# One transfer of 14 rows per partition for W_down in a decode block of attention and a gated feed-forward

## The chip, the cores and the metric

The kernel runs on one core of a Trainium2 chip. A core has a matrix engine (PE, whose weight loads the profile lists apart as PEld), a vector engine (DVE), a scalar engine (ACT), GpSimd (POOL), and a sync engine (SP) that here only starts transfers. Sixteen DMA engines move data between the device memory and the core's on-chip memory, which has 128 partitions. The metric is the device time of one execution in microseconds (us); lower is better. Before the change it is 198.91 us, the median of three runs (198.54 to 199.20).

## The reference

The block adds three things: the input, an attention over a window of a cache, and a gated feed-forward. For four batch rows and one query position each:

```
xn  = layernorm(x)                                  # x: 4 x 512
q   = (xn @ wq) as 32 heads of 128
k,v = the last W = 4096 positions of the caches     # 8 KV heads, 4 query heads each
o   = softmax(q k^T / sqrt(128)) v                  # per batch row and head
A   = o (4 x 4096) @ wo                             # wo: 4096 x 512
B   = (silu(xn @ w_gate) * (xn @ w_up)) @ w_down    # w_gate, w_up: 512 x 1792, w_down: 1792 x 512
out = x + A + B
```

All inputs and the output are bf16. The windows of the two caches are 8 x 4 MB each (4 batch rows, 4096 positions, 128 values), the weights wq and wo 4 MB each, and the three feed-forward matrices 1.75 MB each.

## The kernel before

**The order of the transfers.** SP starts all the large loads on one queue, which the 16 DMA engines work through in order. First come wq, w_gate and w_up, then the keys and values of eight passes, one KV head each for all four batch rows (K0, K1, V0, K2, V1, ... K7, V6, V7), and last w_down and wo. Keys and values have two buffers each: K(r) is started when the transposes of pass r-2 are done (the wait of L232, seen at the start on L233), V(r) when the product with the values of pass r-1 is done (L237, seen on L238). w_down has no wait of its own. It goes into the memory of w_gate and w_up, which were used up at the start. wo goes into the first key buffer in five pieces (`ROWS`: rows 0-15, 16-21, 22-28, 29-30 and 31 of the 32 rows per partition), and its first piece waits until the last keys of that buffer are transposed (L257).

**The start.** While these loads run, DVE and ACT normalize x. PE multiplies by wq (L469), then by w_gate and w_up (L485). PE's result for the feed-forward is laid out in four strips of 32 output partitions, `k` = 0 to 3. Each strip holds up to four tiles of the 1792 hidden values, and the columns of a tile are taken with a stride from the weight's row, because the tile's position on 128 partitions must fit the rows of w_down later. ACT and DVE form silu(gate) * up (L270, L323 to L330), PE transposes the four tiles at once (L490), and DVE copies them into `guT` (L334, L335), which waits in memory for the rest of the kernel. PE goes on to the first pass after `guT` is done (L493).

**A pass.** PE transposes 128 key tiles (L417), DVE and ACT copy them out of PE's result memory (L342, L274), PE forms scores (L426), DVE their maximum (L346), ACT the exponential (L277), PE the sums (L519) and the product with the values (L435).

**The end.** After the last pass PE transposes and regroups the attention's result (L560, L564). Then it adds three products in one result buffer `part_ps`, again in four strips: x, w_down (L574), and the first 22 of 32 row groups of wo (L581). ACT and DVE copy the buffer out (L280, L392), PE folds the four strips into one result (L586) and adds the last ten row groups of wo to it (L593), DVE converts (L394), and SP stores (L260).

**w_down's two parts.** The matrix has 1792 rows = 14 x 128. The kernel before takes the first 1536 rows as 12 rows on each of 128 partitions (`WDA`, one transfer, 12 KB per partition), and the other 256 rows as four rows on each of 64 partitions (`WDB`, two transfers of 32 partitions, 4 KB per partition). So the last strip of the gate and up products has tiles of 64 columns, and the last four products of L574 add over 64 partitions only.

Of the kernel before, what the change touches and what calls it, by code (L numbers as in the profile page):

```python
# [3 lines left out]
BF16 = mybir.dt.bfloat16  # L4
# [6 lines left out]
def bass_parallel_sum__sliding_block_cached__swiglu_ffn__decode_kernel(  # L11
# [12 lines left out]
    B, _, D = A_x.shape  # L24
    _, HKV, Sk, Dh = A_k_cache.shape
    HQ = A_wq.shape[1] // Dh
    F = B_w_gate.shape[1]
# [8 lines left out]
    NC = D // 128  # L36
    NF = F // 128
    REP = HQ // HKV
    CQ = B * REP
    LAST = HKV  # L40

    TA, TB2, PB = 12, 4, 64
    assert 128 * TA + PB * TB2 == F
    SCALE = float(Dh) ** -0.5
    EPS = 1e-5
    BIG = 1.0e30
# [3 lines left out]
    sb = nc.alloc_sbuf_tensor  # L50
# [2 lines left out]
    VB = [sb("vbuf%d" % s, [128, NT, Dh], BF16) for s in range(2)]  # L53
    WG = sb("wg_sb", [128, NC, F], BF16)
    WU = sb("wu_sb", [128, NC, F], BF16)
    WDA = WG[:].rearrange("p c n -> p (c n)")[:, 0:TA * D].rearrange("p (t n) -> p t n", n=D)
    WDB = WU[:].rearrange("p c n -> p (c n)")[:, 0:TB2 * D].rearrange("p (t n) -> p t n", n=D)
    WO = KB[0][:].rearrange("p t d -> p (t d)").rearrange("p (j n) -> p j n", n=D)
    WQ = VB[1][:].rearrange("p t d -> p (t d)").rearrange("p (c n) -> p c n", c=NC)

# [6 lines left out]
    XnT = sb("xnT", [128, NC, 32], BF16)  # L67
# [17 lines left out]
    OT = sb("oT", [128, HKV + 1, CQ], BF16)  # L85
    Rn = sb("rn", [128, 128], BF16)
    OP = sb("oP", [128, 32, 32], BF16)
    guT = sb("guT", [128, TA + TB2, 32], BF16)
    part = sb("part", [128, D], FP32)
    y = sb("y_sb", [128, 128], BF16)  # L90

# [21 lines left out]
    gate_ps = ps_S[2]  # L113
    up_ps = ps_S[3]
    qT_ps = kt_ps[1]
    gT_ps = kt_ps[0][:, 0:4, :]
    part_ps = ps_S[0]
# [4 lines left out]
    def sem(name):  # L122
        return nc.alloc_semaphore(name=name)
# [3 lines left out]
    d_v = [sem("d_v%d" % g) for g in range(2)]  # L127
    d_wg = sem("d_wg")
    d_wu = sem("d_wu")
    d_wda = sem("d_wda")  # L130
    d_wdb = sem("d_wdb")
    d_wo = [sem("d_wo%d" % q) for q in range(len(ROWS))]
    d_out = sem("d_out")
    s_const = sem("s_const")
# [42 lines left out]
    wq_ap = A_wq.rearrange("(p c) n -> p c n", c=NC)  # L177
    wg_ap = B_w_gate.rearrange("(p c) n -> p c n", c=NC)
    wu_ap = B_w_up.rearrange("(p c) n -> p c n", c=NC)
    wda_ap = B_w_down[0:128 * TA, :].rearrange("(p t) n -> p t n", t=TA)  # L180
    wdb_ap = B_w_down[128 * TA:, :].rearrange("(p t) n -> p t n", t=TB2)
    wo_ap = A_wo.rearrange("(p j) n -> p j n", j=32)

    BY_ACT = (4, 7, 8, 11, 12, 14)
# [44 lines left out]
    def run_sync(eng):  # L229
        def load_k(r):  # L230
            if r >= 2:
                eng.wait_ge(s_tr[NCH - 1], r - 1)  # L232
            eng.dma_start(KB[r % 2][:].rearrange("p t d -> p (t d)"), kv_ap(A_k_cache, r)).then_inc(d_k[r % 2], 16)  # L233

        def load_v(r):
            if r:
                eng.wait_ge(s_pv, r)  # L237
            eng.dma_start(VB[r % 2][:].rearrange("p t d -> p (t d)"), kv_ap(A_v_cache, r)).then_inc(d_v[r % 2], 16)  # L238

        eng.dma_start(WQ[:], wq_ap).then_inc(d_v[1], 16)  # L240
        eng.dma_start(WG[:], wg_ap).then_inc(d_wg, 16)
        eng.dma_start(WU[:], wu_ap).then_inc(d_wu, 16)
        load_k(0)
        load_k(1)
        load_v(0)
        for r in range(2, HKV):
            load_k(r)
            load_v(r - 1)
        load_v(HKV - 1)
        eng.dma_start(WDA, wda_ap).then_inc(d_wda, 16)  # L250

        for u in range(0, PB, 32):
            eng.dma_start(WDB[u:u + 32].rearrange("p t n -> p (t n)"),  # L253
                          wdb_ap[u:u + 32].rearrange("(e p) t n -> e p (t n)", p=4)).then_inc(d_wdb, 16)
        for q, (a, b) in enumerate(ROWS):
            if q == 0:
                eng.wait_ge(s_tr[NCH - 1], HKV - 1)  # L257
            eng.dma_start(WO[:, a:b, :], wo_ap[:, a:b, :]).then_inc(d_wo[q], 16)
        eng.wait_ge(s_y, 1)
        eng.dma_start(out_ap, y_ap).then_inc(d_out, 16)  # L260
        eng.wait_ge(d_out, 16)
# [20 lines left out]
    def run_vector(eng):  # L282
# [2 lines left out]
        nc.regs_mov(nx, 0)  # L285
        loc = eng.mark_branch_hint_location()
        eng.memset(XnT[:], 0.0)
        for t in (gate_ps, up_ps):
            eng.memset(t[96:128, :].rearrange("p (t m) -> p t m", m=128)[:, :, PB:], 0.0)
        eng.wait_ge(d_x, 16)  # L290
        eng.tensor_reduce(st_sum[:], X[:], AX.X, ALU.add)
        eng.drain()
# [38 lines left out]
        eng.wait_ge(s_gt, 1)  # L331
        eng.wait_ge(s_fill, 1)
        gT = gT_ps.rearrange("p t (k e) -> p k t e", e=32)
        eng.tensor_copy(guT[:, 0:TA, :].rearrange("p (k t) e -> p k t e", t=4), gT[:, 0:3])  # L334
        eng.tensor_copy(guT[0:PB, TA:, :], gT[0:PB, 3, 0:TB2, :])  # L335
        eng.drain().then_inc(s_guT, 1)
        for t in s_xp + [s_nm]:
            eng.sem_inc(t, 1)
# [57 lines left out]
    def run_tensor(eng):  # L396
        mm = eng.matmul
# [54 lines left out]
        with nc.body("t_head", valid_engines=me):  # L452
            loc = eng.mark_branch_hint_location()
            for t, v in ((nx, 1), (odd, 0), (nk[0], 16), (nk[1], 16)):
                nc.regs_mov(t, v)
            eng.wait_ge(s_c2, 1)
            eng.wait_ge(s_xn, 1)
            for c in range(NC):
                last = eng.transpose(xT_ps[:, c * B:(c + 1) * B],  # L459
                                     xn[:].rearrange("b (p c) -> b c p", c=NC)[:, c, :], ident[0:B, 0:B])  # L460
            last.then_inc(s_xT, 1)
            eng.wait_ge(s_const, 1)
            mm(mask_ps, Lsel[:], Dsh[:])
            eng.wait_ge(s_xnT, 1)
            eng.wait_ge(d_v[1], 16)
            for c in range(NC):
                for j in range(2):
                    for k in range(4):
                        last = mm(ps_S[j][32 * k:32 * k + 32, :], XnT[:, c, :],  # L469
                                  WQ[:, c, 512 * (4 * j + k):512 * (4 * j + k) + 512],  # L470
                                  start=(c == 0), stop=(c == NC - 1), skip_group_check=True)
            last.then_inc(s_q, 1)
            eng.wait_ge(s_qs, 2)
            for j in range(2):
                for h in range(4):
                    last = eng.transpose(qT_ps[:, 4 * j + h, :], qs[:, j, 128 * h:128 * h + 128], ident[:])
            last.then_inc(s_qt, 1)
            for w, d, o, s_w in ((WG, d_wg, gate_ps, s_g), (WU, d_wu, up_ps, s_u)):
                wa = w[:, :, 0:128 * TA].rearrange("p c (m t) -> p c t m", t=TA)
                wb = w[:, :, 128 * TA:].rearrange("p c (m t) -> p c t m", t=TB2)  # L480
                eng.wait_ge(d, 16)
                for c in range(NC):
                    for k in range(4):
                        v = wb[:, c] if k == 3 else wa[:, c, 4 * k:4 * k + 4, :]
                        last = mm(o[32 * k:32 * k + 32, :].rearrange("p (t m) -> p t m", m=128)[:, 0:v.shape[1], 0:v.shape[2]],  # L485
                                  XnT[:, c, :], v, start=(c == 0), stop=(c == NC - 1), skip_group_check=True)
                last.then_inc(s_w, 1)
            eng.wait_ge(s_gu, 1)
            for t in range(4):
                last = eng.transpose(gT_ps[:, t, :], gu[:, 128 * t:128 * t + 128], ident[:])  # L490
            last.then_inc(s_gt, 1)
            eng.wait_ge(s_qc, 1)
            eng.wait_ge(s_guT, 1)  # L493
            nc.br("t_pass", engines=me)
# [20 lines left out]
        with nc.body("t_values", valid_engines=me):  # L515
            j = now(nx)
            for q in range(NB):
                eng.wait_ge(s_xp[q], j)
                last = mm(dn_ps[:], ones[:], P[:, q * TB:(q + 1) * TB, :].rearrange("p t c -> p (t c)"),  # L519
                          start=(q == 0), stop=(q == NB - 1))  # L520
# [11 lines left out]
        with nc.body("t_p_end", valid_engines=me):  # L532
            j = now(nx)
            eng.wait_ge(s_dd, j)
            for q in range(NB):
                mm(S_ps[q], Lsel[:], bc(Dsh[:], TB), start=False, stop=True,  # L536
                   skip_group_check=True).then_inc(s_sh[q], 1)
            eng.wait_ge(s_oc, j)
            for e in range(2):
                last = mm(ot_ps, o4[:, 128 * e:128 * e + 128], fold[:, 16 * e:16 * e + 16],  # L540
                          start=(e == 0), stop=(e == 1), skip_group_check=True)
# [16 lines left out]
        with nc.body("t_tail", valid_engines=me):  # L558
# [3 lines left out]
            for b in range(B):  # L562
                for q in range(4):
                    m = mm(op_ps[:, b, :], sel2[:, b, q, :], Rn[:, 32 * q:32 * q + 32],  # L564
                           start=(b == 0 and q == 0), stop=(q == 3), skip_group_check=True)
            m.then_inc(s_op, 1)
            eng.wait_ge(s_guT, 1)
            eng.wait_ge(d_wda, 16)
            for t in range(TA + TB2):
                k = (t + 1) % 4  # L570
                if t == TA:
                    eng.wait_ge(d_wdb, 16 * (PB // 32))
                a, w = (guT[:, t, :], WDA[:, t, :]) if t < TA else (guT[0:PB, t, :], WDB[0:PB, t - TA, :])
                mm(part_ps[32 * k:32 * k + 32, :], a, w, start=(t < 3), stop=False, skip_group_check=True)  # L574
            eng.wait_ge(s_opc, 1)
            for j in range(EARLY):
                for q, (a, b) in enumerate(ROWS):
                    if a == j:
                        eng.wait_ge(d_wo[q], 16)
                k = (j + 3) % 4  # L580
                m = mm(part_ps[32 * k:32 * k + 32, :], OP[:, j, :], WO[:, j, :], start=False,  # L581
                       stop=(j >= EARLY - 4), skip_group_check=True)
            m.then_inc(s_pt, 1)
            eng.wait_ge(s_ptc, 2)
            for n in range(NC):
                mm(acc_ps[32 * n:32 * n + 32, 0:128], fold[:], part[:, 128 * n:128 * n + 128],  # L586
                   start=True, stop=False, skip_group_check=True)
            for j in range(EARLY, 32):
# [3 lines left out]
                for n in range(NC):  # L592
                    m = mm(acc_ps[32 * n:32 * n + 32, 0:128], OP[:, j, :], WO[:, j, 128 * n:128 * n + 128],  # L593
                           start=False, stop=(j == 31), skip_group_check=True)
# [6 lines left out]
    run_sync(nc.sync)  # L601
    run_scalar(nc.scalar)
    run_vector(nc.vector)
    run_tensor(nc.tensor)


# [26 lines left out]
```

## Time and profile before

| What | Value |
|---|---|
| Median of three runs | 198.91 us (198.54 to 199.20) |
| The profiled execution's own time | 198.22 us |
| Its span (first to last instruction) | 197.0 us |
| Mean granted PE clock | 0.948 of full speed |
| PE busy | 155.0 us (79%) |
| PE weight loads busy | 121.2 us (62%) |
| DVE busy | 114.6 us (58%) |
| ACT busy | 68.8 us (35%) |
| POOL busy | 10.8 us (5%) |
| The SP queue's packets, share of 16 engines' span | 97.0%, 81.01 MB |
| Mean rate of all transfers | 412 GB/s |

The profile is one execution, so stretches of it are compared with its own span; the time of the execution is 1.22 us longer than the span. Line numbers (L574) are those of the kernel before. "Idle" in a row is the time an engine stood still just before, and behind the arrow stands what released it. A busy PE is not PE at its peak, because matmuls are pipelined. In rows of stretches the columns are the length, the busy time and instruction count of each engine, the granted PE clock, the mean busy share of the 16 DMA engines, and the rate that they moved. A packet's busy time runs from its start to its end, so that the share can exceed 1 where packets of one engine overlap.

### The profile page before, as it was taken

What the parts mean: (1) busy time and instruction counts of PE and PEld (TensorE: products, weight loads), DVE (VectorE), ACT (ScalarE), POOL (GpSimd) and SP (SyncE); (2) the same over time, 40 slices, a digit from 0 to 9 for tenths busy, and PEclk for the clock granted to TensorE, in tenths of its full rate; (3) what the DMA queues carried; (4) which work ended last, traced back from release to release, by engine and by line L of the source; (5) the groups of instructions that cost most, each with busy time, mean ns of one, the idle gap of its engine ahead of it and who ended that gap; (6) DMA issues with size and microseconds to landing.
All of it is one profiled execution on the core that took longest, in us unless ns stands there. A gap on an engine that the chain in (4) does not pass through costs nothing.

```text
span 197.0 us, 6539 instructions
## 1 busy us (share of the span) xinstructions
PE 155.0 (79%) x2926; PEld 121.2 (62%) x2926; DVE 114.6 (58%) x218; ACT 68.8 (35%) x86; POOL 10.8 (5%) x27
## 2 busy tenths in 40 slices
PE   0038936998998999899899985998599879988444
PEld 0012106986786888689688954885598568755112
DVE  5472373667667586776768664765376756752201
ACT  2003100470563456057246512652156046430001
POOL 8750000000000000000000000000000000000000
PEclk9999975699999999999999999999799999999957
DMA  6999999999999999999999999999999999999991
GB/s 214 439 427 425 472 453 433 416 433 429 423 423 426 426 426 433 426 426 426 426 439 439 433 439 446 439 426 439 426 433 426 426 426 426 433 411 349 370 400 46
DMA packets 3729, 81.09 MB, mean 412 GB/s; under 512 B 456, under 2 KB 588, under 8 KB 1036
## 3 DMA queue, kind: packets, MB, share of 16 engines
q1 hardware_dynamic: 3716, 81.01, 97.0%
q8 instruction: 5, 0.08, 0.2%
q10 hardware_dynamic: 8, 0.00, 0.0%
HBM read 81.01 MB, written 0.00 MB: 411 GB/s over the span
## 4 chain that ended last, share of the span: by engine, by line
DMA 45%; PE 41%; ACT 7%; DVE 3%; SPq 2%; issue 1%; DVEq 0%
DMA kbuf<-in_A_k_cache_dram 29%; PE ps_kt L417 21%; DMA kbuf<-in_A_wo_dram 15%; PE ps_s L426 9%; ACT kT L274 7%; PE ps_o L435 5%; PE ps_s L536 2%; DVE mxb L346 2%; PE ps_s L581 1%; PE ps_kt L523 1%; PE ps_o L540 1%; DVE mx L369 1%; PE ps_s L593 1%; DVE mxd L371 0%; SPq L253 0%
## 5 line engine op out<-in xcount | busy, mean ns | idle before, releaser
L417 PE MATMUL ps_kt<-ident,kbuf 128*128 128x128 bf16 x1024 | 72.3, 227 | 12.0 <-DMA kbuf<-in_A_k_cache_dram 8.5
L417 PEld LDWEIGHTS ps_kt<-ident,kbuf 128*128 128x128 bf16 x1024 | 61.9, 102 | 19.4 <-DMA kbuf<-in_A_k_cache_dram 9.0
L342 DVE COPY kT<-ps_kt 128x1024 bf16<-128x1024 bf16 x80 | 52.2, 687 | 22.8 <-PE ps_kt L417 21.9
L274 ACT COPY kT<-ps_kt 128x1024 bf16<-128x1024 bf16 x48 | 47.8, 1013 | 47.1 <-PE ps_kt L417 47.1
L277 ACT ACTIVATE p<-ps_s 128x512 bf16<-128x512 f32 x32 | 16.5, 603 | 43.5 <-PE ps_s L536 43.5
L346 DVE TENSOR_REDUCE mxb<-ps_s 128x16 f32<-128x512 f32 x32 | 22.1, 692 | 13.2 <-PE ps_s L426 11.6
L426 PE MATMUL ps_s<-qT,kT 128*128 x1024 | 29.4, 169 | 0.0
L426 PEld LDWEIGHTS ps_s<-qT,kT 128*128 128x128 bf16 x1024 | 27.8, 96 | 0.2
L435 PE MATMUL ps_o<-vbuf,p 128*32 128x256 bf16 x576 | 17.4, 273 | 1.3 <-DMA vbuf<-in_A_v_cache_dram 0.7
L435 PEld LDWEIGHTS ps_o<-vbuf,p 128*32 128x32 bf16 x576 | 15.1, 96 | 2.8 <-issue 2.4
L519 PE MATMUL ps_kt<-p,ones 128*128 128x512 bf16 x36 | 9.7, 378 | 0.2
L536 PE MATMUL ps_s<-dsh,lsel 128*128 128x512 bf16 x36 | 9.4, 382 | 0.0
L350 DVE TENSOR_REDUCE dsum<-ps_kt 128x16 f32<-128x512 f32 x9 | 6.2, 692 | 1.5 <-PE ps_kt L519 1.3
L356 DVE TENSOR_TENSOR oT<-ps_o,rden 128x16 f32 (+1 forms) x9 | 1.6, 175 | 8.9 <-PE ps_o L540 8.9
L469 PE MATMUL ps_s<-vbuf,xnT 128*32 128x512 bf16 x32 | 3.6, 629 | 3.6 <-DMA vbuf<-in_A_wq_dram 3.6
L523 PEld LDWEIGHTS ps_kt<-identf,mxd 128*128 128x128 f32 x9 | 1.2, 138 | 8.2 <-DVEq L372 8.2
L581 PE MATMUL ps_s<-kbuf,oP 128*32 128x512 bf16 x22 | 2.8, 623 | 4.4 <-DMA kbuf<-in_A_wo_dram 4.4
L523 PE MATMUL ps_kt<-identf,mxd 128*128 128x128 f32 x9 | 2.9, 322 | 4.3 <-DVEq L372 4.3
L540 PEld LDWEIGHTS ps_o<-fold,o 128*128 128x128 f32 x36 | 5.4, 190 | 1.3
L280 ACT COPY part<-ps_s 64x512 f32<-64x512 f32 x1 | 0.6, 580 | 14.8 <-PE ps_s L581 14.8
L459 PE MATMUL ps_s<-ident,xn 4*128 4x4 bf16 x4 | 0.3, 166 | 6.9 <-DVE xn L305 6.9
L392 DVE COPY part<-ps_s 64x512 f32<-64x512 f32 x1 | 0.7, 683 | 8.1 <-PE ps_s L581 8.1
(92 smaller groups left out, 77.9 us busy)
## 6 DMA issues: line engine op xcount, KB each, us to landing
kbuf<-in_A_k_cache_dram SPq DMA_DIRECT2D x8, 4096.0 KB, 26.9
vbuf<-in_A_v_cache_dram SPq DMA_DIRECT2D x8, 4096.0 KB, 28.8
vbuf<-in_A_wq_dram SPq DMA_DIRECT2D x1, 4096.0 KB, 12.3
kbuf<-in_A_wo_dram SPq DMA_DIRECT2D x1, 2048.0 KB, 30.4
wg_sb<-in_B_w_gate_dram SPq DMA_DIRECT2D x1, 1792.0 KB, 16.2
wu_sb<-in_B_w_up_dram SPq DMA_DIRECT2D x1, 1792.0 KB, 20.0
wg_sb<-in_B_w_down_dram SPq DMA_DIRECT2D x1, 1536.0 KB, 26.1
kbuf<-in_A_wo_dram SPq DMA_DIRECT2D x1, 896.0 KB, 33.5
```

The costliest lines, as they stand in the source:

```text
L274: eng.copy(KT[n % 8][:], kt_ps[n % 3]).then_inc(s_ev[n], 1)
L277: eng.activation(P[:, q * TB:(q + 1) * TB, :], S_ps[q], ACT.Exp, scale=SCALE).then_inc(s_xp[q], 1)
L342: eng.tensor_copy(KT[n % 8][:], kt_ps[n % 3]).then_inc(s_ev[n], 1)
L346: eng.tensor_reduce(mxb[:, q, :], S_ps[q].rearrange("p t c -> p c t"), AX.X, ALU.max)
L350: eng.tensor_reduce(dsum[:], dn_ps[:].rearrange("p (t c) -> p c t", c=CQ), AX.X, ALU.add)
L417: last = eng.transpose(kt_ps[n % 3][:, k, :], KB[g][:, 8 * n + k, :], ident[:])
L426: last = mm(S_ps[q][:, 8 * (n % 4) + k, :], KT[n % 8][:, k, :], QT[:, bass.ds(j, 1), :, :].rearrange("p o b h -> p (o b h)"), start=(n % 4 ...
L435: last = mm(o4_ps[32 * k:32 * k + 32, :], P[:, 2 * u:2 * u + 2, :].rearrange("p t c -> p (t c)"), VB[e][:, 2 * u:2 * u + 2, :].rearrange(" ...
L519: last = mm(dn_ps[:], ones[:], P[:, q * TB:(q + 1) * TB, :].rearrange("p t c -> p (t c)"), start=(q == 0), stop=(q == NB - 1))
L523: eng.transpose(mx_ps, mxd[:], identf[:]).then_inc(s_mt, 1)
L536: mm(S_ps[q], Lsel[:], bc(Dsh[:], TB), start=False, stop=True, skip_group_check=True).then_inc(s_sh[q], 1)
L540: last = mm(ot_ps, o4[:, 128 * e:128 * e + 128], fold[:, 16 * e:16 * e + 16], start=(e == 0), stop=(e == 1), skip_group_check=True)
```

## The change

w_down becomes one transfer: partition p takes the rows 14p to 14p+13, 14 KB in one piece, into the memory of w_gate alone. The two transfers onto 64 partitions and their semaphore are gone, and the 16 matmuls of L574 (12 over 128 partitions and 4 over 64) become 14 over 128.

The columns of the gate and up products follow: a tile is now every 14th column. The four strips take tiles 0-3, 4-7, 8-11 and 10-13, so that the last strip has 512 columns in place of 256 and computes tiles 10 and 11 a second time. DVE's two clears of the unused part of that strip (L289) are gone, and the second copy into `guT` takes the strip's last two tiles on 128 partitions in place of four tiles on 64.

```diff
-    TA, TB2, PB = 12, 4, 64
+    NF = F // 128
+    T0 = (0, 4, 8, NF - 4)
-    WDA = WG[:].rearrange("p c n -> p (c n)")[:, 0:TA * D].rearrange("p (t n) -> p t n", n=D)
-    WDB = WU[:].rearrange("p c n -> p (c n)")[:, 0:TB2 * D].rearrange("p (t n) -> p t n", n=D)
+    WD = WG[:].rearrange("p c n -> p (c n)").rearrange("p (t n) -> p t n", n=D)
-    wda_ap = B_w_down[0:128 * TA, :].rearrange("(p t) n -> p t n", t=TA)
-    wdb_ap = B_w_down[128 * TA:, :].rearrange("(p t) n -> p t n", t=TB2)
+    wd_ap = B_w_down.rearrange("(p t) n -> p t n", t=NF)
...
-        eng.dma_start(WDA, wda_ap).then_inc(d_wda, 16)
-        for u in range(0, PB, 32):
-            eng.dma_start(WDB[u:u + 32].rearrange("p t n -> p (t n)"),
-                          wdb_ap[u:u + 32].rearrange("(e p) t n -> e p (t n)", p=4)).then_inc(d_wdb, 16)
+        eng.dma_start(WD, wd_ap).then_inc(d_wd, 16)
...
-        for t in (gate_ps, up_ps):
-            eng.memset(t[96:128, :].rearrange("p (t m) -> p t m", m=128)[:, :, PB:], 0.0)
...
-        eng.tensor_copy(guT[:, 0:TA, :].rearrange("p (k t) e -> p k t e", t=4), gT[:, 0:3])
-        eng.tensor_copy(guT[0:PB, TA:, :], gT[0:PB, 3, 0:TB2, :])
+        eng.tensor_copy(guT[:, 0:12, :].rearrange("p (k t) e -> p k t e", t=4), gT[:, 0:3])
+        eng.tensor_copy(guT[:, 12:NF, :], gT[:, 3, 16 - NF:, :])
...
-                wa = w[:, :, 0:128 * TA].rearrange("p c (m t) -> p c t m", t=TA)
-                wb = w[:, :, 128 * TA:].rearrange("p c (m t) -> p c t m", t=TB2)
+                wt = w[:].rearrange("p c (m t) -> p c t m", t=NF)
...
-                        v = wb[:, c] if k == 3 else wa[:, c, 4 * k:4 * k + 4, :]
-                        last = mm(o[32 * k:32 * k + 32, :].rearrange("p (t m) -> p t m", m=128)[:, 0:v.shape[1], 0:v.shape[2]],
-                                  XnT[:, c, :], v, start=(c == 0), stop=(c == NC - 1), skip_group_check=True)
+                        last = mm(o[32 * k:32 * k + 32, :].rearrange("p (t m) -> p t m", m=128), XnT[:, c, :],
+                                  wt[:, c, T0[k]:T0[k] + 4, :], start=(c == 0), stop=(c == NC - 1), skip_group_check=True)
...
-            eng.wait_ge(d_wda, 16)
-            for t in range(TA + TB2):
+            eng.wait_ge(d_wd, 16)
+            for t in range(NF):
                 k = (t + 1) % 4
-                if t == TA:
-                    eng.wait_ge(d_wdb, 16 * (PB // 32))
-                a, w = (guT[:, t, :], WDA[:, t, :]) if t < TA else (guT[0:PB, t, :], WDB[0:PB, t - TA, :])
-                mm(part_ps[32 * k:32 * k + 32, :], a, w, start=(t < 3), stop=False, skip_group_check=True)
+                mm(part_ps[32 * k:32 * k + 32, :], guT[:, t, :], WD[:, t, :], start=(t < 3), stop=False,
+                   skip_group_check=True)
```

The order of SP's starts at the end of the kernel before, from V6 and V7 (L238) to the pieces of wo (L258); `wg_sb` and `wu_sb` are the memories of w_gate and w_up, and the shape behind a row is partitions x values:

```order
L238 DMA vbuf<-in_A_v_cache_dram 128x1x16384 x2
L250 DMA wg_sb<-in_B_w_down_dram 128x6144
L253 DMA wu_sb<-in_B_w_down_dram 32x2048 x2
L258 DMA kbuf<-in_A_wo_dram 128x8192
L258 DMA kbuf<-in_A_wo_dram 128x3072
L258 DMA kbuf<-in_A_wo_dram 128x3584
```

The same place after the change:

```order
L234 DMA vbuf<-in_A_v_cache_dram 128x1x16384 x2
L246 DMA wg_sb<-in_B_w_down_dram 128x7168
L250 DMA kbuf<-in_A_wo_dram 128x8192
L250 DMA kbuf<-in_A_wo_dram 128x3072
L250 DMA kbuf<-in_A_wo_dram 128x3584
```

Between the last values and the first piece of wo there is one start in place of three; the bytes are the same.

PE's matmuls at the end of the kernel before, from the transpose of the attention's result (L560) to the last rows of wo (L593):

```order
L560 MATMUL ps_kt<-ident,oT 128x128
L564 MATMUL ps_s<-rn,sel 128x32 x16
L574 MATMUL ps_s<-wg_sb,guT 32x512 x12
L574 MATMUL ps_s<-wu_sb,guT 32x512 x4
L581 MATMUL ps_s<-kbuf,oP 32x512 x22
L586 MATMUL ps_s<-part,fold 32x128 x4
L593 MATMUL ps_s<-kbuf,oP 32x128 x40
```

The same place after the change:

```order
L548 MATMUL ps_kt<-ident,oT 128x128
L552 MATMUL ps_s<-rn,sel 128x32 x16
L559 MATMUL ps_s<-wg_sb,guT 32x512 x14
L567 MATMUL ps_s<-kbuf,oP 32x512 x22
L572 MATMUL ps_s<-part,fold 32x128 x4
L579 MATMUL ps_s<-kbuf,oP 32x128 x40
```

The product with w_down is two matmuls shorter and reads one memory, behind one wait instead of two; nothing else has moved on PE.

More of the change, by code (lines that the diff above doesn't have):

```diff
@@ L40, in bass_parallel_sum__sliding_block_cached__swiglu_ffn__decode_kernel @@
     LAST = HKV
-    TA, TB2, PB = 12, 4, 64
-    assert 128 * TA + PB * TB2 == F
+    NF = F // 128
+    T0 = (0, 4, 8, NF - 4)
     SCALE = float(Dh) ** -0.5
@@ L87, in bass_parallel_sum__sliding_block_cached__swiglu_ffn__decode_kernel @@
     OP = sb("oP", [128, 32, 32], BF16)
-    guT = sb("guT", [128, TA + TB2, 32], BF16)
+    guT = sb("guT", [128, NF, 32], BF16)
     part = sb("part", [128, D], FP32)
@@ L129, in bass_parallel_sum__sliding_block_cached__swiglu_ffn__decode_kernel @@
     d_wu = sem("d_wu")
-    d_wda = sem("d_wda")
-    d_wdb = sem("d_wdb")
+    d_wd = sem("d_wd")
     d_wo = [sem("d_wo%d" % q) for q in range(len(ROWS))]
```

## The prediction

> **What bounds the kernel now.** I read the page first (the 40 slices and the chain), then the stretches of the end, then the transfers of single stretches. The slices say that the 16 DMA engines hardly rest:
>
> ```profile
> DMA  6999999999999999999999999999999999999991
> GB/s 214 439 427 425 472 453 433 416 433 429 423 423 426 426 426 433 426 426 426 426 439 439 433 439 446 439 426 439 426 433 426 426 426 426 433 411 349 370 400 46
> DMA 45%; PE 41%; ACT 7%; DVE 3%; SPq 2%; issue 1%; DVEq 0%
> ```
>
> A slice is 4.9 us. The rate stands near 426 GB/s for most of the kernel and falls in the last ones, to 349 and 370, although the engines stay 90% busy. The chain (third row) gives PE 41%, but it follows one path through a pipeline in which a pass of PE hides behind the transfers of the next; what all passes share is one queue that is never empty. So a byte saved or a stall removed on that queue should show, if the end of the kernel waits for it. Whether it does stands in the order of time:
>
> ```profile
> 178.95 1.93 PE L435 MATMUL ps_o<-vbuf,p 128*32 128x256 bf16 x64 [0.73 <-DMA vbuf<-in_A_v_cache_dram]
> 183.03 0.56 PE L564 MATMUL ps_s<-rn,sel 128*128 128x32 bf16 x16 [0.32 <-DVE rn L388]
> 183.77 0.83 PE L574 MATMUL ps_s<-wg_sb,guT 128*32 128x512 bf16 x12 [0.17 <-DMA wg_sb<-in_B_w_down_dram]
> 184.76 0.40 PE L574 MATMUL ps_s<-wu_sb,guT 64*32 64x512 bf16 x4 [0.17 <-DMA wu_sb<-in_B_w_down_dram]
> 189.59 2.82 PE L581 MATMUL ps_s<-kbuf,oP 128*32 128x512 bf16 x22 [4.42 <-DMA kbuf<-in_A_wo_dram]
> 191.37 0.13 PEld L581 LDWEIGHTS ps_s<-kbuf,oP 128*32 128x32 bf16 x6 [0.79 <-DMA kbuf<-in_A_wo_dram]
> 193.55 1.12 PEld L593 LDWEIGHTS ps_s<-kbuf,oP 128*32 128x32 bf16 x40 [0.17 <-DMA kbuf<-in_A_wo_dram]
> ```
>
> PE waits for the last values, then for w_down (by 0.17 us), and then 4.42 us for the first piece of wo, 0.79 us for the second and 0.17 us for the third. From 185.16 to the end the pace is that of wo's landing. w_down lies ahead of wo in the same queue, so what w_down costs the queue is passed on whole.
>
> **What w_down costs the queue.** Four stretches: the steady part, the arrival of w_down's first part, the five microseconds behind it, and one of wo alone.
>
> ```profile
> 160.00:176.00 16.00, 14.91 (x322) 12.45 (x320) 11.77 (x22) 6.38 (x7) 0.00 (x0) 1.00 0.99 428
> 176.00:180.00 4.00, 3.06 (x50) 1.88 (x53) 1.12 (x3) 1.66 (x4) 0.00 (x0) 1.00 0.92 387
> 180.00:185.00 5.00, 4.34 (x77) 2.53 (x66) 1.56 (x4) 0.00 (x0) 0.00 (x0) 1.00 1.04 316
> 185.00:189.00 4.00, 0.16 (x4) 0.00 (x0) 0.00 (x0) 0.00 (x0) 0.00 (x0) 0.84 0.96 403
> ```
>
> The last two numbers are DMA share and rate. From 180 to 185 us the engines are fully occupied (1.04) and move 316 GB/s, where they move 428 with as much occupation before. They don't lack work; each packet takes longer. The packets of three pieces of this stretch, 180 to 182, 182 to 185 and 185 to 186.8:
>
> ```profile
> DMA packets 106, 0.54 MB, mean 272 GB/s; under 512 B 35, under 2 KB 35, under 8 KB 82
> DMA packets 88, 1.04 MB, mean 345 GB/s; under 512 B 12, under 2 KB 12, under 8 KB 28
> DMA packets 47, 0.77 MB, mean 428 GB/s; under 512 B 0, under 2 KB 0, under 8 KB 0
> ```
>
> Between 2 and 8 KB lie 82-35 = 47 packets in the first and 28-12 = 16 in the second: 63 of the 64 packets of 4 KB that two transfers onto 32 partitions make. Where there are most, the rate is lowest (272); where there are some, 345; where there are none and the engines read wo alone, it is back at 428. So the slow stretch belongs to the 4 KB packets onto the 64 partitions, not to wo.
>
> **The change part by part.** (1) The queue. The same 1792 KB go out, in packets of 14 KB on all partitions; those of 4 KB vanish. The price of the slow stretch, first way: (428-316)/428 x 5 us = 1.31 us. Second way, by landings:
>
> ```profile
> 159.06 30.39 DMA kbuf<-in_A_wo_dram
> kbuf<-in_A_wo_dram SPq DMA_DIRECT2D x1, 2048.0 KB, 30.4
> wg_sb<-in_B_w_down_dram SPq DMA_DIRECT2D x1, 1536.0 KB, 26.1
> wu_sb<-in_B_w_down_dram SPq DMA_DIRECT2D x2, 128.0 KB, 25.0
> ```
>
> wo's first piece lands at 159.06+30.39 = 189.45, the last values at about 178.9 (PE's wait above ends there). Between the two go 1536+2x128+2048 = 3840 KB, 3.93 MB, in 10.55 us. At 428 GB/s they need 9.19, so 1.36 us are lost on the way to the landing that PE waits for. Both ways agree. The bounds: if 428 is too much for packets this small and 403 (the row of 185 to 189) is right, 3.93 MB need 9.76 us and 0.8 us are lost. Upward: from 176 to 180 the rate is 387, and with (428-387)/428 x 4 = 0.38 us added to 1.31 it is 1.7. The new packets have their like in this trace: w_gate and w_up are 14 KB on each of 128 partitions too, and the stretch in which they land shows no slow place:
>
> ```profile
> 13.00:21.00 8.00, 6.85 (x54) 2.29 (x56) 1.49 (x6) 1.87 (x2) 0.00 (x0) 1.00 1.07 457
> ```
>
> I take 1.3 us saved, bounds 0.7 to 1.7; the 0.7 is the first rival's.
>
> [...]
>
> (2) SP. Two starts fall away:
>
> ```profile
> 158.12 0.89 SPq L253 DMA_DIRECT2D wu_sb<-in_B_w_down_dram  x2
> 159.06 2.32 SPq L258 DMA_DIRECT2D kbuf<-in_A_wo_dram  x5
> ```
>
> wo's starts move up by 0.94 us, worth nothing: they land 30 us later, so they wait behind the queue. Without that cover (an empty queue) they would be worth the 0.94 us.
>
> (3) PE at the end. 14 matmuls at 0.83/12 = 0.069 us take 0.97 us, from 183.77 to 184.74. All of them now wait for the whole of w_down. Its 1792 KB need 4.29 us from 178.9, so it lands near 183.2, ahead of L564's end at 183.59. Behind this wait stands L581, which needs wo at about 189.45-1.3 = 188.15; so there are 3.4 us of cover, and the 0.4 us that PE ends earlier are worth nothing either.
>
> (4) After that, everything moves with wo. The second piece (L581's last six), the two copies, the fold and L593 keep their lengths, and each of the landings that start them comes 1.3 us earlier. L593 depends on wo's third piece and its last rows, all behind the same place in the queue. Half clock in the tail stays in the forecast (below).
>
> (5) The start. The last strip reads 512 columns in place of 256, in gate and up:
>
> ```profile
> L485 PE MATMUL ps_s<-wg_sb,xnT 128*32 128x512 bf16 x12 | 3.8, 1076 | 0.0
> L485 PE MATMUL ps_s<-wg_sb,xnT 128*32 128x256 bf16 x4 | 1.1, 414 | 0.0
> 29.14 0.21 DVE L335 COPY guT<-ps_kt 64x128 bf16<-64x128 bf16 x1
> 31.49 4.77 PE L417 MATMUL ps_kt<-ident,kbuf 128*128 128x128 bf16 x43 [2.67 <-DMA kbuf<-in_A_k_cache_dram]
> kbuf<-in_A_k_cache_dram SPq DMA_DIRECT2D x1, 4096.0 KB, 18.1
> 1.22 0.55 DVE L289 MEMSET ps_s<- 32x256 f32 x2
> ```
>
> Below: nothing, where the four strips run beside each other (12 of 1.08 us fit in 3.8). Above: 4 x (1076-414) = 2.65 us for each of the two. By columns it is 3.8 x (2048-1792)/1792 = 0.54 us each, and I take that. `guT` is ready at 29.35, the keys come at 31.49; so 2.1 us are covered. If the upper end came true for both (5.3 us), the first pass would start 3.2 us late at most, and the cover behind that is the queue: the keys started between 44 and 46 us (fifth row) land 18.1 us later though their 4.19 MB need 9.8, so they have 8.3 us of other bytes ahead. The longer stride (14 in place of 12 values) lies in the same bounds. The two clears on DVE (0.55 us, last row) lie ahead of its wait for x, and the copies keep their size. All of this: 0.
>
> Sum: -1.3 us. The profiled execution's span of 197.0 becomes 195.7, its own time of 198.22 becomes 196.9. The median of the runs is 0.69 us above that execution, so for the median I forecast 198.91-1.3 = **197.6 us**.
>
> **The rivals.** *Half of it.* Only the 4 KB packets themselves are slow, and the rest of the slow stretch is the switch from one kind of packet to the next, which stays. Then the gain is what the two microseconds with most of them lose, (428-272)/428 x 2 = 0.7 us: 198.2. For it speaks that the stretch from 182 to 185 us holds few 4 KB packets at 345 GB/s; against it the landing of wo, 1.36 us late. *Nothing.* The slow stretch is wo's start, 16 KB out of each 32 KB, and it stays: 198.9. Against it speaks 272 GB/s where the 4 KB packets are most, and 428 at 185 with wo alone. *Clock.* PE runs at half clock for the whole tail:
>
> ```profile
> 187.00:188.00 1.00, 0.00 (x0) 0.00 (x0) 0.00 (x0) 0.00 (x0) 0.00 (x0) 0.85 1.00 414
> 189.00:190.00 1.00, 0.41 (x8) 0.20 (x12) 0.00 (x0) 0.00 (x0) 0.00 (x0) 0.50 1.03 427
> 192.00:194.00 2.00, 1.22 (x26) 0.65 (x28) 0.68 (x1) 0.58 (x1) 0.00 (x0) 0.50 0.28 106
> kbuf<-in_A_wo_dram SPq DMA_DIRECT2D x1, 128.0 KB, 33.6
> q8 instruction: 5, 0.08, 0.2%
> ```
>
> It falls at about 187.7, in the idle time from 185.16 to 189.59 (4.4 us), which becomes 3.4. If the clock stays up, L593 (1.19 us) halves; the last row of wo (started near 160.9, landed 33.6 later at 194.5, L593's end 194.8) allows 0.3 us of that: 197.3. [...] *Slower.* From 192 to 194 the share is 0.28: about four engines of 16 still run when the others are done, some 1.6 us behind. The trace counts five instruction fetches on these engines (last row, 0.08 MB). PE's program gets shorter, so the fetches may fall otherwise. If one hits an engine that is late already, the last landing comes another 1.6 us later, and with 1.3 saved the time is 199.2. It decides as soon as such a lag exceeds 1.3 us. [...]
>
> **How the numbers follow.** Forecast 0.74, half 0.10, nothing 0.07, clock 0.05, slower 0.04. The forecast's own range by its bounds is 197.2 to 198.2. For 8 in 10 I take 197.0 to 198.5, which holds the half and the clock too and leaves out nothing and slower, with some of the forecast for the spread of the medians (0.3 us either way). What can be told from no change is 0.3%, 0.6 us: below 198.3 counts as faster. The forecast and the clock lie below it, the half close under it, of which I count 0.07: faster 0.86. Nothing, the rest of the half, and a slower case that stays under 199.5: same 0.11. Slower 0.03.
>
> **What would show it.** Right: no packets between 2 and 8 KB before wo's second piece, a rate near 428 in the five microseconds after 180, wo's first piece landing at 188.1, PE's wait for it near 3.4 us, and L593 starting at 192.2. Wrong: a rate of 316 without 4 KB packets (nothing), or PE still waiting for wo's last rows after 193.5 with a faster stretch before (slower). A first transpose of keys after 31.5 would make step 5 wrong, and the span would tell whether the queue covered it.

## The result and the profile after

The changed kernel takes 196.7 us (median of five runs, 196.56 to 196.72), the kernel before 198.9 us (median of five, 198.48 to 199.20). The ratio is 0.9898, 95% interval 0.9885 to 0.9911: 2.2 us faster, outside the forecast range on the fast side. The profiled executions stand closer together than the medians:

| | Before | After | Forecast |
|---|---|---|---|
| Median of the runs | 198.9 us | 196.7 us | 197.6 us |
| The profiled execution's own time | 198.22 us | 196.72 us | 196.9 us |
| Its span | 197.0 us | 195.5 us | 195.7 us |

So the forecast for the profiled execution is 0.2 us off, and that for the median 0.9 us. What follows asks where those 0.7 us lie.

The slices of the changed kernel, its page's rows on the transfers: the rate no longer falls to 349 and 370 near the end.

```profile
DMA  6999999999999999999999999999999999999991
GB/s 222 429 428 428 451 436 429 426 439 436 419 443 419 431 436 443 429 436 436 429 429 436 429 429 429 429 429 429 429 429 436 429 429 429 429 429 404 413 404 51
```

The stretches of the end of the changed kernel, with DMA share and rate last, and then the packets from 180 to 182 and from 182 to 185 us:

```profile
160.00:176.00 16.00, 14.73 (x320) 12.34 (x318) 11.68 (x22) 6.52 (x8) 0.00 (x0) 1.00 0.99 426
180.00:185.00 5.00, 4.07 (x68) 2.32 (x56) 1.55 (x4) 0.00 (x0) 0.00 (x0) 0.99 1.00 424
185.00:189.00 4.00, 0.99 (x12) 0.53 (x16) 0.00 (x0) 0.00 (x0) 0.00 (x0) 0.50 0.99 411
192.00:194.00 2.00, 1.33 (x48) 1.07 (x40) 0.29 (x1) 0.00 (x0) 0.00 (x0) 0.50 0.03 10
...
DMA packets 69, 0.88 MB, mean 438 GB/s; under 512 B 12, under 2 KB 12, under 8 KB 12
DMA packets 80, 1.25 MB, mean 415 GB/s; under 512 B 4, under 2 KB 4, under 8 KB 4
```

From 180 to 185 the rate is 424 in place of 316 GB/s at full occupation, and no packet between 2 and 8 KB is left (12-12 and 4-4). In order of time, PE's last values, w_down, wo's pieces, and the end:

```profile
178.78 1.93 PE L425 MATMUL ps_o<-vbuf,p 128*32 128x256 bf16 x64 [0.71 <-DMA vbuf<-in_A_v_cache_dram]
183.35 1.04 PE L559 MATMUL ps_s<-wg_sb,guT 128*32 128x512 bf16 x14
188.00 2.82 PE L567 MATMUL ps_s<-kbuf,oP 128*32 128x512 bf16 x22 [3.61 <-DMA kbuf<-in_A_wo_dram]
189.79 0.13 PEld L567 LDWEIGHTS ps_s<-kbuf,oP 128*32 128x32 bf16 x6 [0.80 <-DMA kbuf<-in_A_wo_dram]
191.99 1.14 PEld L579 LDWEIGHTS ps_s<-kbuf,oP 128*32 128x32 bf16 x40 [0.17 <-DMA kbuf<-in_A_wo_dram]
193.70 0.69 SPq L252 DMA_DIRECT2D out_dram<-y_sb  x1
```

From the start of the product with the last values to that of the product with wo pass 188.00-178.78 = 9.22 us; before the change 189.59-178.95 = 10.64. These 1.42 us are, up to 0.1 us, all that separates the two profiled executions (198.22-196.72 = 1.50). Behind wo's first piece the rows have the lengths and waits that they had before (2.82 us, 0.80, 0.17).

### The profile page after: what moved, and what is told of

Its sections match the earlier page's. It is cut to its first block, busy times and chain, and to the rows that moved or that the text cites. A ratio compares the mean times of both kernels' runs of the same rounds, so it can differ in the third digit from the quotient of the medians.

```text
span 195.5 us, 6522 instructions
## 1 busy us (share of the span) xinstructions
PE 153.8 (79%) x2915; PEld 119.9 (61%) x2924; DVE 114.0 (58%) x216; ACT 68.8 (35%) x86; POOL 10.5 (5%) x27
## 4 chain that ended last, share of the span: by engine, by line
DMA 44%; PE 40%; ACT 7%; DVE 4%; issue 2%; SPq 1%; DVEq 0%
DMA kbuf<-in_A_k_cache_dram 29%; PE ps_kt L407 20%; DMA kbuf<-in_A_wo_dram 15%; PE ps_s L416 9%; ACT kT L266 7%; PE ps_o L425 5%; PE ps_s L524 2%; DVE mxb L336 2%; PE ps_s L567 1%; PE ps_kt L511 1%; PE ps_o L528 1%; DVE mx L359 1%; PE ps_s L579 1%; DVE mxd L361 0%; DVE kT L332 0%
## 5 line engine op out<-in xcount | busy, mean ns | idle before, releaser
L407 PE MATMUL ps_kt<-ident,kbuf 128*128 128x128 bf16 x1024 | 71.4, 226 | 10.6 <-DMA kbuf<-in_A_k_cache_dram 6.6
L407 PEld LDWEIGHTS ps_kt<-ident,kbuf 128*128 128x128 bf16 x1024 | 60.7, 101 | 18.3 <-DMA kbuf<-in_A_k_cache_dram 7.2
L507 PE MATMUL ps_kt<-p,ones 128*128 128x512 bf16 x27 | 7.6, 379 | 0.9 <-ACT p L269 0.2
L344 DVE COPY o<-ps_o 128x256 f32<-128x256 f32 x9 | 3.8, 425 | 2.5 <-PE ps_o L425 2.0
```

Of the source, the lines that this page charges most:

```text
L407: last = eng.transpose(kt_ps[n % 3][:, k, :], KB[g][:, 8 * n + k, :], ident[:])
```

## The experiments

Each kernel is the kernel before or the changed kernel with the edit shown. The times of the kernel before beside them are 198.67 us (23 runs) in the first group, 198.62 (21 runs) in the second, and 198.73 (19 runs) in the third; each group ran on a chip of its own. The changed kernel was not run again, so where its 196.7 us stands beside a run of the second or third group, the comparison crosses groups.

### The kernel before, once more

No edit.

> The kernel before, unchanged, once more. Its median was 198.9 us but its profiled execution 198.22, and the change moved the median by 2.2 us and the profiled execution by 1.5. If the cost of the slow stretch at 180 to 185 us differs from execution to execution (theory 1), this kernel's times spread over 0.5 us or more again, and a new profile shows a stretch that loses another amount than 1.3 us. If the profiled execution was low for another reason, for one the PE clock in the tail (theory 2), the stretch loses 1.3 us again and the difference lies behind 189 us.

Measured: 198.62 us, median of 12 runs (198.32 to 199.04), and 198.67 in the 23 runs beside it (197.95 to 199.31). Of these 35 executions only two are as fast as 198.22, the profiled one that the forecast was made from. The spans of all 35 reach from 196.7 to 198.1 us with a median of 197.4, where the first profile has 197.0; the five of the changed kernel reach from 195.3 to 195.5. The new profile, of an execution of 198.54 us:

```profile
180.00:185.00 5.00, 3.98 (x66) 2.29 (x58) 1.54 (x4) 0.00 (x0) 0.00 (x0) 1.00 1.04 270
...
178.83 1.93 PE L435 MATMUL ps_o<-vbuf,p 128*32 128x256 bf16 x64
189.90 2.81 PE L581 MATMUL ps_s<-kbuf,oP 128*32 128x512 bf16 x22 [4.50 <-DMA kbuf<-in_A_wo_dram]
```

The slow stretch moves 270 GB/s where the first profile has 316. Against the 426 GB/s of this profile's steady part it loses (426-270)/426 x 5 = 1.83 us, and from the values to wo pass 11.07 us. Behind it the two profiles are alike: from the start of wo's product to the start of the store pass 5.60 us here and 5.59 in the first profile. So theory 1: the cost of the slow stretch differs from execution to execution, and the execution that was read is a cheap one.

### Two rows on each of 128 partitions

```diff
-    TA, TB2, PB = 12, 4, 64
+    TA, TB2, PB = 12, 2, 128
...
-        for u in range(0, PB, 32):
-            eng.dma_start(WDB[u:u + 32].rearrange("p t n -> p (t n)"),
-                          wdb_ap[u:u + 32].rearrange("(e p) t n -> e p (t n)", p=4)).then_inc(d_wdb, 16)
+        eng.dma_start(WDB, wdb_ap).then_inc(d_wdb, 16)
...
```

> w_down still in two parts and in two memories, but the last 256 rows go as 2 rows onto each of 128 partitions, in packets of 2 KB. The start keeps 256 columns in the last strip. Theory A, all 16 DMA engines write into too few partitions: the slow stretch is gone though the packets are smaller still, time within 0.3 us of the changed kernel (196.7). Theory B, small packets are slow in themselves: twice as many packets of half the size, 198.9 or more. Theory C, the gain of 2.2 us has a part in the start or in the shorter product with w_down: about 197.3.

Measured: 196.65 us (196.55 to 196.83), ratio to before 0.9900, interval 0.9883 to 0.9917. The packets of 2 KB cost nothing:

```profile
180.00:185.00 5.00, 4.18 (x72) 2.43 (x61) 1.55 (x4) 0.00 (x0) 0.00 (x0) 1.00 1.03 432
...
178.90 1.93 PE L433 MATMUL ps_o<-vbuf,p 128*32 128x256 bf16 x64 [0.84 <-DMA vbuf<-in_A_v_cache_dram]
188.19 2.83 PE L579 MATMUL ps_s<-kbuf,oP 128*32 128x512 bf16 x22 [3.69 <-DMA kbuf<-in_A_wo_dram]
```

This kernel still has two parts, two memories and 256 columns in the last strip of gate and up. It has the whole gain, so neither small packets nor the start nor one memory in place of two is its cause. Theory B falls, and C as far as the start goes; the product with w_down has 14 matmuls here too, and w_down has two transfers in place of three, so on these two points the next pair decides. It also decides whether theory A must be about the number of partitions or about their place.

### The same packets on other partitions

Both kernels keep four rows on 64 partitions, in one transfer, and multiply over all 128 partitions with zeros outside; they differ in the partitions alone.

```diff
-        for u in range(0, PB, 32):
-            eng.dma_start(WDB[u:u + 32].rearrange("p t n -> p (t n)"),
-                          wdb_ap[u:u + 32].rearrange("(e p) t n -> e p (t n)", p=4)).then_inc(d_wdb, 16)
+        eng.dma_start(WDB[32:32 + PB].rearrange("p t n -> p (t n)"),
+                      wdb_ap.rearrange("(e p) t n -> e p (t n)", p=4)).then_inc(d_wdb, 16)
...
```

In the second kernel the first index is 0 in place of 32.

> The last 256 rows as 4 rows on 64 partitions as before, but on partitions 32 to 95 and in one transfer, the same 64 packets of 4 KB. The product with w_down runs over 128 partitions, zeros outside. [...] If 64 partitions are too few wherever they lie, or packets of 4 KB are slow: 198.9, like the run on partitions 0 to 63.

> The twin of the run on partitions 32 to 95: the same single transfer and the same products over 128 partitions, but on partitions 0 to 63. [...] If two transfers in place of one were the cost: 196.7 to 197.0.

Measured: partitions 32 to 95 take 196.63 us (196.55 to 196.83; ratio 0.9903, interval 0.9886 to 0.9920), partitions 0 to 63 take 198.65 us (198.19 to 198.95; ratio 0.9999, 0.9985 to 1.0013). First partitions 32 to 95, then in a fence of its own 0 to 63:

```profile
180.00:185.00 5.00, 3.95 (x66) 2.20 (x54) 1.55 (x4) 0.00 (x0) 0.00 (x0) 1.00 1.05 441
...
DMA packets 127, 0.88 MB, mean 442 GB/s; under 512 B 27, under 2 KB 27, under 8 KB 84
...
178.66 1.93 PE L434 MATMUL ps_o<-vbuf,p 128*32 128x256 bf16 x64 [0.72 <-DMA vbuf<-in_A_v_cache_dram]
187.92 2.83 PE L581 MATMUL ps_s<-kbuf,oP 128*32 128x512 bf16 x22 [3.65 <-DMA kbuf<-in_A_wo_dram]
```

```profile
180.00:185.00 5.00, 3.89 (x65) 2.22 (x54) 1.54 (x4) 0.00 (x0) 0.00 (x0) 1.00 1.03 273
...
DMA packets 87, 0.48 MB, mean 240 GB/s; under 512 B 21, under 2 KB 21, under 8 KB 67
...
178.74 1.93 PE L434 MATMUL ps_o<-vbuf,p 128*32 128x256 bf16 x64 [0.83 <-DMA vbuf<-in_A_v_cache_dram]
189.97 2.83 PE L581 MATMUL ps_s<-kbuf,oP 128*32 128x512 bf16 x22 [4.36 <-DMA kbuf<-in_A_wo_dram]
```

The packet rows are of 180 to 182 us: 84-27 = 57 packets of 4 KB go at 442 GB/s on partitions 32 to 95, and 67-21 = 46 go at 240 on 0 to 63. Same bytes, same packets, same products; the place alone is worth 2.0 us. The run on 32 to 95 has the whole gain with 16 matmuls, and the run on 0 to 63 has none of it with one transfer in place of two, so neither of these two things is the cause. Nor is it the number of partitions, which is 64 in both. Why 0 to 63 lose and 32 to 95 do not is not shown.

### How much a transfer onto partitions 0 to 63 costs

The changed kernel gets one more transfer behind w_down that nobody reads, into the memory of w_up; the store's wait at the end also waits for it.

```diff
         eng.dma_start(WD, wd_ap).then_inc(d_wd, 16)
+        eng.dma_start(WU[:].rearrange("p c n -> p (c n)")[0:64, 0:4 * D],
+                      B_w_down[0:64 * 4, :].rearrange("(e p t) n -> e p (t n)", p=4, t=4)).then_inc(d_more, 16)
...
```

The others have two rows on 128 partitions, twelve rows on 64, or the first one's transfer between the keys of pass 5 and the values of pass 4.

> The changed kernel with one more transfer behind w_down that nobody reads: 256 KB onto partitions 0 to 63 (64 packets of 4 KB, into the memory of w_up). At the steady rate (428 GB/s) these bytes alone cost 0.6 us: 197.3. Theory P, only these packets move at half rate: 0.6 us on top, 197.9. Theory Q, they slow the packets of the other engines as well, as before the change: 2.0 us on top, 199.3.

> The control: the changed kernel with the same 256 KB more onto 128 partitions, 2 KB each. Both theories: the bytes alone, 0.6 us, 197.3.

> Three times the amount onto partitions 0 to 63 (64 packets of 12 KB). The bytes alone cost 1.84 us: 198.5. Theory P, half rate for them: 1.84 us on top, 200.4. Theory Q with a cost that grows with the amount, 3 x 2.0 us on top: 204.5. Theory Q with a cost per transfer, whatever its size: 2.0 us on top, 200.5; then the trace tells it from P by the rate of wo's first packets.

> The transfer of the first of these runs, 256 KB onto partitions 0 to 63, but in the middle of the kernel, between the keys of pass 5 and the values of pass 4, among packets of 32 KB. If the queue bounds the kernel everywhere, the price is that of the end: 199.3 by theory Q, 197.9 by theory P. If the middle has slack, 196.7.

| More bytes | Median (runs) | Above the changed kernel | On top of the bytes at 428 GB/s |
|---|---|---|---|
| 256 KB on 128 partitions | 197.41 us (197.21 to 198.06) | 0.7 us | 0.1 us |
| 256 KB on partitions 0 to 63 | 199.52 us (199.18 to 200.08) | 2.8 us | 2.2 us |
| 768 KB on partitions 0 to 63 | 203.11 us (202.82 to 204.46) | 6.4 us | 4.6 us |
| 256 KB on 0 to 63, in mid-kernel | 199.38 us (199.03 to 200.43) | 2.7 us | 2.1 us |

Theory Q holds: 256 KB cost 2.1 us more on 64 partitions than on 128 (199.52-197.41), where half rate for them alone would be 0.6 (an estimate: 256 KB at 428 GB/s once more). In neither form is it right for the larger amount: three times the bytes cost twice as much, 4.6 us, more than a cost per transfer (2.0) and less than one that grows in proportion (6). Half rate for 768 KB (1.84 us) is short by a factor of 2.5. In mid-kernel the price is the same, so the queue bounds there too. That place, from 117 to 122 us, and the steady part behind it:

```profile
117.00:122.00 5.00, 1.56 (x19) 0.91 (x8) 0.84 (x3) 2.06 (x4) 0.00 (x0) 1.00 1.13 315
124.00:140.00 16.00, 14.78 (x308) 12.93 (x306) 10.59 (x20) 6.71 (x8) 0.00 (x0) 0.92 1.00 430
```

For 768 KB the slow stretch lasts nine microseconds, at a share near 1, and is over when the rate is back (third row):

```profile
180.00:185.00 5.00, 3.21 (x58) 2.10 (x46) 1.54 (x4) 0.00 (x0) 0.00 (x0) 0.94 1.11 240
185.00:189.00 4.00, 1.89 (x14) 0.53 (x14) 0.00 (x0) 0.00 (x0) 0.00 (x0) 0.50 0.89 205
189.00:192.00 3.00, 0.00 (x0) 0.00 (x0) 0.00 (x0) 0.00 (x0) 0.00 (x0) 0.50 0.99 421
```

205 GB/s over four microseconds is just under half of 428; in the part from 182 to 185 it is 187.

Which packets are slow can be read from the single packets of the kept traces. A packet of 4 KB takes 0.16 us on average and one of 12 KB 0.47 in the run on 32 to 95, one of 14 KB 0.54 and one of 16 KB 0.62 in the changed kernel. What the packets take beyond that, added up and divided by the 16 engines, in us:

| Profile | The packets onto 64 partitions | w_down's other packets, started ahead of them | wo's first piece, started behind them | Sum |
|---|---|---|---|---|
| Before, first profile | 0.23 | 0.22 | 0.94 | 1.39 |
| 4 KB packets on 0 to 63 | 0.40 | 0.34 | 1.18 | 1.92 |
| 256 KB more on 0 to 63 | 0.40 | 0.36 | 1.17 | 1.93 |
| 768 KB more on 0 to 63 | 2.08 | 0.49 | 1.71 | 4.28 |

The sums come close to the losses in time (1.4, 2.0, 2.1 and 4.6 us), and for 256 KB four fifths of them lie in packets that go to all 128 partitions. wo's packets of 16 KB, 0.62 us otherwise, take up to 1.35 us in the first profile. In the run on 32 to 95 no packet of w_down or of wo's first piece takes more than 0.01 us beyond its average.

### 256 KB in two transfers onto 32 partitions each

Two transfers of 128 KB onto 32 partitions each, behind w_down of the changed kernel, onto 0 to 31 and 64 to 95 or onto 0 to 31 and 32 to 63:

```diff
         eng.dma_start(WD, wd_ap).then_inc(d_wd, 16)
+        eng.dma_start(WU[:].rearrange("p c n -> p (c n)")[0:0 + 32, 0:4 * D],
+                      B_w_down[0:0 + 128, :].rearrange("(e p t) n -> e p (t n)", p=4, t=4)).then_inc(d_more, 16)
+        eng.dma_start(WU[:].rearrange("p c n -> p (c n)")[64:64 + 32, 0:4 * D],
+                      B_w_down[128:128 + 128, :].rearrange("(e p t) n -> e p (t n)", p=4, t=4)).then_inc(d_more, 16)
...
```

> The changed kernel with 256 KB more that nobody reads, in two transfers of 32 partitions: 0 to 31 and 64 to 95. [...]

> The same two transfers of 32 partitions as the kernel before had them, 0 to 31 and 32 to 63, behind the changed kernel's w_down. [...]

Measured: 198.75 us (198.37 to 199.44) for 0 to 31 and 64 to 95, 199.57 us (199.11 to 200.62) for 0 to 31 and 32 to 63. The second is the time of one transfer onto 0 to 63: two transfers or one make no difference (199.52). The first falls between that and the same bytes on 128 partitions: 1.3 us of the loss remain (198.75-197.41), and 0.8 us are gone. The slow stretch of the first is there, less deep (319 GB/s, where the second has 283):

```profile
180.00:185.00 5.00, 3.87 (x74) 2.60 (x68) 1.54 (x4) 0.00 (x0) 0.00 (x0) 1.00 1.01 319
```

The packets' sum, as in the table above, is 1.26 us. So a transfer onto 0 to 31 and one onto 64 to 95 still lose 1.3 us, while the one transfer of w_down's last 256 rows onto 32 to 95 lost nothing (196.63 us). What the remaining 1.3 us belong to, these runs don't show.

## Why the prediction was wrong, point by point

**What bounds the kernel** was right. 256 KB more on all partitions cost 0.7 us, near their 0.6 us at the steady rate, and the price of the transfer onto 0 to 63 is nearly the same in mid-kernel as at the end (2.1 and 2.2 us on top of its bytes).

**The slow stretch belongs to the 4 KB packets on the 64 partitions** was right as to the place and left open as to the reason. The runs separate it: on partitions 32 to 95 these packets go at full rate (441 GB/s from 180 to 185 us), and packets half as large on 128 partitions do too (432). It is the partitions (273 on 0 to 63). But "not to wo" holds for the cause only: of the 1.39 us by which this profile's packets are longer, 0.94 lie in wo's packets and 0.23 in the 4 KB ones.

**The step that failed is the last one of the sum**: "The median of the runs is 0.69 us above that execution, so for the median I forecast 198.91-1.3". It takes the 0.69 us as an offset that stays. Some 0.4 us of it are stall that the profiled execution happened to have less of, and the change takes the whole stall away: its span is 197.0 against a median of 197.4, and in the second profile of the same kernel the interval below is 0.43 us longer. The other 0.2 to 0.3 us lie in the three first runs, whose median of 198.91 is above the medians of 198.62 to 198.73 that 75 later executions gave; why is not shown. The interval from the product with the last values to that with wo, in the profiled executions of five kernels shown above, one of them twice, against their own times:

| Kernel | Time | Interval | Time less interval |
|---|---|---|---|
| Before, first profile | 198.22 us | 10.64 us | 187.58 us |
| Before, second profile | 198.54 us | 11.07 us | 187.47 us |
| 4 KB packets on 0 to 63 | 198.70 us | 11.23 us | 187.47 us |
| Changed | 196.72 us | 9.22 us | 187.50 us |
| Two rows on 128 | 196.83 us | 9.29 us | 187.54 us |
| 4 KB packets on 32 to 95 | 196.56 us | 9.26 us | 187.30 us |

The last column is constant to 0.3 us, so the interval carries both the gain and the spread of the kernel before. Without the stall it is 9.2 to 9.3 us, close to the 9.19 us that the prediction worked out from bytes and rate. With it, it is 10.64 to 11.23: a loss of 1.4 to 2.0 us. A median of 198.9 us would go with an interval of about 11.4 (198.9-187.5) and a loss of 2.2, but of such an execution there is no profile. The term was "1.3 us saved, bounds 0.7 to 1.7". For the execution that it was read from it was right: the interval became 1.42 us shorter. For the median it measured 2.2, and 2.0 to 2.1 in the three pairs of runs that differ in the partitions alone or nearly so. The bounds came from one execution's rates and could not hold what other executions add: the mechanism was right, and its size was that of a cheap execution. The times before did show a hint: the three runs spread over 0.66 us and the profiled execution lay under all of them. After the change five runs lie within 0.16 us.

**SP's two starts: nothing** and **PE at the end: nothing** were right. With one start fewer the run on 0 to 63 gained nothing, and with all 16 matmuls the run on 32 to 95 has the whole gain. PE's 14 matmuls start at 183.35 with no wait for w_down and take 1.04 us (0.97 forecast); then PE stands still for 3.61 us (3.4 forecast). **Everything moves with wo** was right: wo's product starts at 188.00 (landing forecast at 188.1) and the last ten row groups at 191.99 (192.2).

**The start: nothing** was right. The gate's row before the change, and then the changed kernel's rows for gate, the last copy into `guT`, and the first transposes:

```profile
18.30 3.78 PE L485 MATMUL ps_s<-wg_sb,xnT 128*32 128x512 bf16 x16
...
18.60 3.87 PE L473 MATMUL ps_s<-wg_sb,xnT 128*32 128x512 bf16 x16
29.52 0.18 DVE L325 COPY guT<-ps_kt 128x64 bf16<-128x64 bf16 x1
31.36 2.85 PE L407 MATMUL ps_kt<-ident,kbuf 128*128 128x128 bf16 x25 [2.15 <-DMA kbuf<-in_A_k_cache_dram]
```

The gate's product takes 3.87 us, 0.09 more than before rather than the 0.54 that I took. So the lower bound of step 5 came true, which fits strips that run beside each other; no run varies it alone. `guT` is ready at 29.70 in place of 29.35, still ahead of the keys, and 0.30 us of the delay of 0.35 are there already when gate starts (18.60 against 18.30).

**The rivals.** *Half of it* and *nothing* are out: the rate is 424 with wo's start in place. *Slower* did not come; from 192 to 194 the DMA share is 0.03. *Clock*: the tail of the changed kernel ran at half clock (0.50 in its rows above), and that of two of the experiments came out of it, with the last stretch and the store first of the run with two rows on 128 and then of that on 32 to 95:

```profile
192.00:194.00 2.00, 1.29 (x48) 0.62 (x40) 0.29 (x1) 0.00 (x0) 0.00 (x0) 1.00 0.05 17
...
193.80 0.69 SPq L258 DMA_DIRECT2D out_dram<-y_sb  x1
```

```profile
192.00:194.00 2.00, 1.01 (x40) 0.52 (x37) 0.29 (x1) 0.00 (x0) 0.00 (x0) 1.00 0.04 13
...
193.54 0.69 SPq L259 DMA_DIRECT2D out_dram<-y_sb  x1
```

From the start of wo's product to the start of the store pass 5.61 (193.80-188.19) and 5.62 us (193.54-187.92) with the clock back, and 5.70 (193.70-188.00) at half clock. What the clock is worth in this tail is about 0.1 us, and the 0.9 us are not there.

## What to carry to other kernels

Where transfers bound a kernel, look for stretches in which the DMA engines are fully occupied and move fewer bytes, and ask which partitions the packets of that stretch go to; the place on the partitions was worth 2.0 us here at the same bytes and packets. Here the stall was a spread too (spans of 196.7 to 198.1 us with it, 195.3 to 195.5 without): one profile prices it for one execution, and an offset between that execution and the median may be the stall itself, so the range for removing it should reach at least to the stall plus that offset. Where 64 partitions are all there is, try other ones, in one transfer: 32 to 95 took 196.63 us here, 0 to 63 took 198.65.

## What the runs showed that was not expected

A transfer onto partitions 0 to 63 cost far more than half rate for its own bytes: 2.1 us for 256 KB and 4.6 us for 768 KB, against 0.6 and 1.84, which are estimated from 428 GB/s. While it lasts, the packets of w_down and wo beside it are slowed as well, and for 256 KB they hold most of the loss (1.53 of 1.93 us). Two transfers onto 0 to 31 and 64 to 95 in place of that one remove only 0.8 of the 2.1 us. Why it costs this much, why 32 to 95 cost nothing, and what sets its size in one execution (10.64 to 11.23 us of interval for the same packets), stays open: the runs varied place and amount, but not when the single engines reach the transfer.
